# Two decode blocks on one core: eight units of K held over between the layers, and the weights in between streamed as one array

## The chip, the cores and the metric

The kernel runs on one core of a Trainium2 chip. The metric is the device time of one execution in microseconds (us); lower is better. The kernel before takes 2557.58 us, the median of three runs (2556.99 to 2559.53).

## The reference, cut to what matters

```python
def A(x, k_cache, v_cache, wq, wo):        # x (2, 1, 512); caches (2, 8, 32768, 128); all float32
    q = heads of x @ wq                    # 32 heads of 128; 4 heads share one K/V head
    p = softmax(q @ k_cache.T * 128 ** -0.5)
    return (p @ v_cache).reshape(2, 1, 4096) @ wo
def B(x, w_gate, w_up, w_down):            # 512 -> 1792 -> 512
    return (gelu(x @ w_gate) * (x @ w_up)) @ w_down
x = x + A(layernorm(x)); x = x + B(layernorm(x))
x = x + A(layernorm(x)); x = x + B(layernorm(x))     # the same caches and weights again
```

Both layers read the same K and V caches (268 MB each) and the same weights. One token per batch row is computed, so nearly all the work is reading.

## The kernel before

All data pass through one SBUF array, `mem`, of `UNITS` = 110 units. A **unit** is 512 float32 columns on 128 partitions: 262,144 bytes. Units 0 to 31 are region A, 32 to 63 region B, 64 to 95 region C, and 96 to 109 are the **room**. One (K/V head, batch row) pair has 64 units of K and 64 of V, and they are loaded as halves of 32 units. There are 16 pairs to a layer; the second layer visits them in reverse, so that the last pair of layer 0 is the first of layer 1.

All loads are issued on SP's queue from one list, `stream`, in the order in which it is filled. `plan` gives each load a fixed place in `mem`; `pump` (the DMA is line 487) issues the head of the list whenever its place is free; `done` and `give` free places as TensorE (PE) finishes with them. The wait of an SP instruction is thus a wait for the last reader of its place, and whatever is behind it in the list waits too. Line 716 is the score matmul, 782 the value matmul, 676 the query projection, 901 the gate/up matmul, 886 and 829 the down projection (829 also the last head of the output projection), and 641 (`warm`) a matmul on constants.

At the turn between the layers the last pair is not loaded again in full. Its V stays (64 units in B and C), its first 32 units of K stay in A, and `stash` (line 737) copies the last `WAIT` = 6 units of K out of region B into six PSUM banks, three copies on ScalarE (ACT) and three on VectorE (DVE), and `scores` copies them back to A (line 728) once part of A has been used. The other 26 units are loaded a second time:

```python
K_PARTS = [{}, {ORDER[-1]: [(32, 3), (35, 3), (38, 4), (42, 4), (46, 4), (50, 8)],   # (first unit, units)
```

Since A, B and C are full of kept data, everything between the layers goes through the room: the last 4 units of `wo`, gate and up (28 units in 8 pieces), `wd` (14 units in 4 pieces), `wq` of layer 1 (32 units in 10 pieces) and the first four K pieces. They rotate over four places of 3, 4, 3 and 4 units, so a piece can be issued when PE has used the piece four before it. Unit 96 is held for one half of the softmax result until `leave()`, after the values of the last pair. At the end of layer 1, regions A and C are free, and the 42 remaining units of weights are loaded ahead in larger pieces.

The last pair of a layer ends in `combine` (lines 793 and 794): ACT scales columns 0 to 255 of A's bank and DVE columns 256 to 511.

Of the kernel before, what the change touches and what calls it, by code (L numbers as in the profile page):

```python
# [12 lines left out]
OP = mybir.AluOpType  # L13
# [11 lines left out]
FH = 2 * KC * sum(FW)  # L25
FD = DF // P
HALF = 2048
# [21 lines left out]
BACK = A_AT + 13  # L49

K_PARTS = [{}, {ORDER[-1]: [(32, 3), (35, 3), (38, 4), (42, 4), (46, 4), (50, 8)],
# [7 lines left out]
WO_PARTS = [[(0, 28), (28, 4)], [(4, 28), (0, 4)]]  # L59
# [21 lines left out]

def plan():
# [12 lines left out]
    put("k", 1, last, [107, 96, 99, 103, A_AT, A_AT + 4])  # L95
# [3 lines left out]
    out["wq", 0, 0] = C_AT  # L99
    for i in range(10):  # L100
        out["wd", 0, i] = out["wq", 1, i] = [103, 106, 96, 99][i % 4]
    for i in range(8):
        out["gu", 0, i] = [103, 106.5, 96, 99][i % 4]
    out["wo", 0, 0] = out["wo", 1, 0] = C_AT
    out["wo", 0, 1] = 99
    out["wo", 1, 1] = 106
    for i, o in zip((0, 1, 4, 5, 6), (A_AT, A_AT + 7, A_AT + 14, A_AT + 21, A_AT + 24.5)):
        out["gu", 1, i] = o
    for i, o in enumerate((A_AT + 28, 97, 100, 104, C_AT)):
        out["wd", 1, i] = o  # L110
    return out
# [322 lines left out]
def block_kernel(nc, x, kt, vt, wq, wo, gu, wd, out):  # L434
# [76 lines left out]

    def meets(l, n):
        return (l == 0 and n == len(ORDER) - 1), (l == 1 and n == 0)
# [8 lines left out]
    for l in range(2):  # L522
        for i, (s, m) in enumerate(pieces(WQ_SPLIT[l])):
            add(("wq", l, i), wq[:, s * DM:(s + m) * DM], m * DM)
# [23 lines left out]
        if not l:  # L548
            add_wo(l, 1)
        for e in range(2):  # L550
            half_of = gu[e * P * FH:(e + 1) * P * FH].rearrange("(p c) -> p c", p=P)
            for j, (c, m) in enumerate(pieces(GU_SPLIT[l][e])):
                add(("gu", l, KC * e + j), half_of[:, c:c + m], m)
        for j, (o, m) in enumerate(pieces(WD_SPLIT[l])):
            add(("wd", l, j), wd[:, o * DM:(o + m) * DM], m * DM)
# [114 lines left out]
    def queries(l):  # L670
        qp = small(A)
        for j, (s, m) in enumerate(pieces(WQ_SPLIT[l])):
            w = get(("wq", l, j), m)
            for i in range(s, s + m):
                (k, v), t = divmod(i // 4, 2), i % 4
                pe.matmul(qp[32 * t:32 * t + 32, :], window(k, v), w[:, i - s, :],  # L676
                          start=(i < 4), stop=(i >= 8 * KC - 4))
                if i == 2:
                    spread(W if l else A)
            done(("wq", l, j))  # L680
            if l and j != len(WQ_SPLIT[l]) - 2:
                warm(256, W)
        for i in range(0, 512, 256):
# [14 lines left out]
    def scores(l, n, g, b):  # L698
# [3 lines left out]
        if second:  # L702
            todo = [(("k", 0, g, b, 0), s, s, m) for s, m in pieces(STEPS)] + [(None, BACK, 2 * CHUNK - WAIT, WAIT)]
        else:
            todo = []
        todo += [(("k", l, g, b, s), 0, s, m) for s, m in (parts if second else sorted_parts)("k", l, (g, b))]
        order = [j for key, o, s, m in todo for j in range(s, s + m)]
        for key, o, s, m in todo:
# [11 lines left out]
            if first:  # L720
                if s:
                    done(key, 0, m - WAIT)
# [108 lines left out]
    def last_head(l, g):  # L831
        s, m = WO_PARTS[l][1]
        w = get(("wo", l, 1), m)
# [21 lines left out]
    def feedforward(l):  # L855
# [22 lines left out]
        def down(j, n, m):  # L878
            w = get(("wd", l, j), m)
            for i in range(n, n + m):  # L880
                e, r = divmod(i, FD // 2)
                t, c = divmod(r, nj)
                h = hT[:, nj * e + c, t, :]
                if i < tops:
                    q = i % 4
                    pe.matmul(W[32 * q:32 * q + NB, :], h, w[:, i - n, :], start=(i < 4), stop=(i + 4 >= tops))
                    continue
                add_row(h, w[:, i - n, :], i == FD - 1)
            done(("wd", l, j))

        tops = sum(WD_SPLIT[l][:1 if l else 2])
        for e in range(2):
            for i, (s, m) in enumerate(pieces(GU_SPLIT[l][e])):
                key = "gu", l, KC * e + i
                w = flat_of(key)
                c = 0
                for k in range(KC):
                    for t, n in enumerate(FW):
                        if s <= c < s + m:
                            o = both[e][32 * t:32 * t + 32, :].rearrange("p (x c) -> p x c", x=2)[:, :, :n]  # L900
                            pe.matmul(o, window(k, 0), w[:, c - s:c - s + 2 * n].rearrange("p (x c) -> p x c", x=2),
                                      start=(k == 0), stop=(k == KC - 1))
                        c += 2 * n
                done(key)
                if e == i == 0:
                    spread(A)
                    rstd = state["rstd"]
                    hrr, cube, root = (tiny(n) for n in ("hrr", "cube", "root"))
                    dve.scalar_tensor_tensor(hrr, rstd, 0.5, rstd, op0=OP.mult, op1=OP.mult)
                    dve.tensor_scalar(cube, rstd, math.sqrt(0.044715), None, op0=OP.mult)  # L910
                    dve.tensor_scalar(root, rstd, math.sqrt(2.0 / math.pi), None, op0=OP.mult)
                if e and s + m == FH // 2:
                    hidden(0)
                if s + m == FH:
                    gelu(e)
                if e:
                    warm(256, W[:NB])
        n = 0
        for j, m in enumerate(WD_SPLIT[l]):
            if l and j == 1:  # L920
                hidden(1)
                turn(state["x"], side())
            elif not l and 1 <= j <= 2:
                if j == 1:
                    warm(256)
                    hidden(1)
                else:
                    warm(512)
                    turn(xin, side())
            down(j, n, m)  # L930
            n += m
# [51 lines left out]
_INS = ["x", "kt", "vt", "wq", "wo", "gu", "wd"]  # L983
# [6 lines left out]
def halves(gate, up):  # L990
    out = []
    for e in range(2):
        c, cols = e * DF // 2, []
        for n in FW:
            cols += [gate[:, c:c + n], up[:, c:c + n]]
            c += n
        w = np.concatenate(cols, axis=1).reshape(KC, P, -1).transpose(1, 0, 2)
        out.append(np.ascontiguousarray(w).reshape(-1))
    return np.concatenate(out)
# [27 lines left out]
```

## Time and profile before

| | |
|---|---|
| median of three runs | 2557.58 us |
| the profiled execution, whole | 2557.27 us |
| its span, first to last instruction | 2555.8 us |
| PE, DVE, ACT busy | 1228.2, 145.8, 81.4 us |
| read from HBM | 1102.58 MB, 431 GB/s over the span |
| DMA queue of SP | 99.9% of 16 engines' span |

The profile has one execution. Its span is 1.5 us shorter than that execution's time, and the execution is 0.3 us under the median. "DMA share" in the views below is the mean busy share of the core's 16 DMA engines; packets that overlap let it go a little above 1.

### The profile page before, as it was taken

To read this page: it belongs to the slowest core of one execution; us is meant where nothing else is said; L and a number is where in the kernel's file an instruction comes from. 1 tells how busy PE (TensorE), PEld (TensorE's weight loads), DVE (VectorE), ACT (ScalarE), POOL (GpSimd) and SP (SyncE) were. 2 spreads that over 40 slices of the span, in tenths; PEclk is the share of its full clock that TensorE was granted. 3 is DMA by queue.
4 is the path that set the end of the run, shared out by engine and by line. 5 is a ranking of instruction groups with operands and counts; after the bars stand their busy time and mean duration, and the time that the engine had idled before them with its cause. 6 is when DMAs were issued, how large, how long until landed. Compare 5 with 4: busy or idle time off the path is not lost.

```text
span 2555.8 us, 19801 instructions
## 1 busy us (share of the span) xinstructions
PE 1228.2 (48%) x9177; PEld 320.9 (13%) x9177; DVE 145.8 (6%) x495; ACT 81.4 (3%) x189; POOL 2.7 (0%) x9
## 2 busy tenths in 40 slices
PE   3444445354455354354684553544544544534456
PEld 1011111011011011111121110111111111101112
DVE  0000000000000000000010000000000000000001
ACT  0000000000000000000000000000000000000000
POOL 0000000000000000000000000000000000000000
PEclk8677777777777777776897767777777777767788
DMA  9999999999999999999999999999999999999999
GB/s 426 428 439 431 435 432 431 438 432 437 431 431 436 432 437 431 435 432 431 427 418 436 434 433 436 433 433 434 431 437 432 435 433 432 435 433 434 434 433 386
DMA packets 25091, 1102.91 MB, mean 432 GB/s; under 512 B 2792, under 2 KB 2928, under 8 KB 5616
## 3 DMA queue, kind: packets, MB, share of 16 engines
q1 hardware_dynamic: 25056, 1102.65, 99.9%
q8 instruction: 12, 0.20, 0.0%
q14 instruction: 7, 0.06, 0.0%
q10 hardware_dynamic: 16, 0.00, 0.0%
HBM read 1102.58 MB, written 0.07 MB: 431 GB/s over the span
## 4 chain that ended last, share of the span: by engine, by line
DMA 74%; PE 23%; SPq 1%; another core or an unknown queue 0%; DVE 0%; issue 0%; ACT 0%
DMA mem<-in_kt 37%; DMA mem<-in_vt 35%; PE S L716 12%; PE A L782 11%; DMA mem<-in_wd 1%; SPq L487 1%; DMA mem<-in_wq 1%; DMA mem<-in_gu 1%; PE A L676 0%; PE W L829 0%; PE A L716 0%; ACT T L753 0%; DVE desk L755 0%; DVE aux L719 0%
## 5 line engine op out<-in xcount | busy, mean ns | idle before, releaser
L716 PE MATMUL S<-mem,aux 128*32 128x512 f32 x4032 | 512.1, 666 | 617.3 <-DMA mem<-in_kt 617.3
L782 PE MATMUL A<-mem 128*16 128x512 f32 x2048 | 292.3, 732 | 477.6 <-DMA mem<-in_vt 477.6
L782 PE MATMUL A<-mem,desk 128*16 128x512 f32 x2048 | 286.2, 722 | 32.4 <-DMA mem<-in_vt 17.7
L716 PEld LDWEIGHTS S<-mem,aux 128*32 128x32 f32 x4032 | 133.7, 121 | 972.6 <-DMA mem<-in_kt 639.7
L782 PEld LDWEIGHTS A<-mem 128*16 128x16 f32 x2048 | 62.2, 113 | 705.5 <-DMA mem<-in_vt 507.6
L719 DVE TENSOR_REDUCE aux<-S 128x1 f32<-128x512 f32 x63 | 43.5, 691 | 1130.7 <-PE S L716 1130.7
L782 PEld LDWEIGHTS A<-mem,desk 128*16 128x16 f32 x2048 | 64.6, 111 | 227.4 <-issue 209.4
L753 ACT ACTIVATE T<-S,aux 128x512 f32<-128x512 f32 x63 | 41.4, 657 | 1196.7 <-DVE aux L749 1196.7
L759 PE MATMUL M<-aux 128*128 128x4 f32 x64 | 14.5, 298 | 85.2 <-DVE aux L757 85.2
L798 ACT ACTIVATE desk<-A,aux 128x512 f32<-128x512 f32 x30 | 20.6, 687 | 1072.2 <-PE A L782 1072.2
L803 DVE TENSOR_REDUCE aux<-A 128x4 f32<-128x64 f32 x16 | 3.6, 226 | 551.8 <-PE A L801 551.8
L803 DVE TENSOR_REDUCE aux<-M 128x4 f32<-128x64 f32 x16 | 3.6, 226 | 512.6 <-PE M L801 512.6
L746 PE MATMUL M<-aux 128*128 128x128 f32 x32 | 10.3, 323 | 34.5 <-DVE aux L744 34.5
L755 DVE STREAM_TRANSPOSE desk<-T 128x512 f32<-128x512 f32 x32 | 22.9, 716 | 27.0 <-ACT T L753 27.0
L759 PEld LDWEIGHTS M<-aux 128*128 128x128 f32 x64 | 11.7, 229 | 91.3 <-DVE aux L757 91.3
L755 DVE STREAM_TRANSPOSE mem<-T 128x512 f32<-128x512 f32 x32 | 22.9, 717 | 0.0
L811 PE MATMUL W<-mem,aux 128*2 128x512 f32 x112 | 16.8, 765 | 12.4 <-DMA mem<-in_wo 12.4
L641 PE MATMUL W<-aux 128*128 128x256 f32 (+3 forms) x58 | 18.0, 392 | 1.0 <-DVE W L876 0.7
L676 PE MATMUL M<-mem,aux 128*32 128x512 f32 x64 | 9.5, 669 | 18.0 <-DMA mem<-in_wq 18.0
L801 PE MATMUL A<-aux,desk 128*128 128x128 f32 x64 | 10.1, 280 | 14.6 <-ACT desk L798 13.7
L801 PE MATMUL M<-aux,desk 128*128 128x128 f32 x64 | 10.7, 287 | 12.8 <-ACT desk L798 12.3
L753 ACT ACTIVATION_READ_ACCUMULATOR T<-S,aux 128x1 f32 x63 | 12.4, 196 | 0.0
(136 smaller groups left out, 191.5 us busy)
## 6 DMA issues: line engine op xcount, KB each, us to landing
mem<-in_wo SPq DMA_DIRECT2D x2, 7168.0 KB
mem<-in_vt SPq DMA_DIRECT2D x3, 4096.0 KB, 20.0
mem<-in_vt SPq DMA_DIRECT2D x1, 6144.0 KB, 29.2
mem<-in_gu SPq DMA_DIRECT2D x6, 896.0 KB, 28.2
mem<-in_gu SPq DMA_DIRECT2D x3, 1792.0 KB, 40.2
mem<-in_kt SPq DMA_DIRECT2D x1, 4864.0 KB, 17.6
mem<-in_vt SPq DMA_DIRECT2D x2, 2048.0 KB, 32.4
mem<-in_wd SPq DMA_DIRECT2D x4, 1024.0 KB, 21.6
```

The source lines that it names most:

```text
L487: sp.dma_start(at[key][1], src, sem=(key[0], key[4]) if plain else "any")
L641: pe.matmul(bank, ident[:, :bank.shape[0]], part.to_broadcast([P, n]), start=alone, stop=alone)
L716: pe.matmul(banks[u][32 * t:32 * t + 32, :], pad[:, PAD_Q - 4 * c:PAD_Q + 32 - 4 * c], w[:, j - s, :], start=(j == tile_of[0]), stop=(j == ...
L719: dve.tensor_reduce(mx[:, u:u + 1], banks[u], axis=AX.X, op=OP.max)
L746: pe.transpose(m[:, :P], nm.to_broadcast([P, P]), ident)
L753: act.activation(T[u], banks[u], AF.Exp, bias=bias, scale=SCALE, accum_out=ls[:, u:u + 1])
L755: dve.transpose(p[u], T[u])
L759: pe.matmul(m[:, :REP], both.to_broadcast([P, P]), same, start=True, stop=True)
L782: pe.matmul(A[32 * t:32 * t + 16, :], p[u][:, at_p:at_p + 16], w[:, QUAD * i + t, :], start=(j == order[0]), stop=(j == order[-1]))
L798: act.activation(desk, A, AF.Copy, scale=linv)
L801: pe.transpose(m[:, c * P:(c + 1) * P], desk[:, c * P:(c + 1) * P], ident)
L811: pe.matmul(W[32 * t:32 * t + NB, :], heads(g)[:, t, :], w[:, REP * g + t - s, :], start=(g == turns[0]), stop=(g == turns[-1]))
```

## The change

- `stash` keeps eight units of K instead of six: the last `SPARES` = 2 units of `mem` (108 and 109) take two, copied from SBUF to SBUF, PSUM the other six. It makes eight copies, four on each engine, over two engines.
- The room that the pieces rotate in has `ROOM` = 12 units, in four places of 3. The second load of K is 24 units, as 3, 3, 3, 3, 4 and 8.
- The last four units of `wo`, gate/up, `wd` and `wq` become one array in HBM, `ws`, of 78 units a row. Between the layers it is read as 26 pieces of 3 units that pay no heed to where one matrix ends; the query weights at the very start come from it too. Gate and up are cut into units of 512 columns (`GU_UNITS`), in which the last, narrower block of two k-steps shares a unit.
- At the end of layer 1 the ten pieces are 7, 7, 7, 4, 3, 4, 3, 4, 2, 1 units (before 7, 7, 7, 3.5, 3.5, 4, 3, 4, 2, 1).
- `combine` for the last pair splits by partitions instead of columns: ACT takes 0 to 63, DVE 64 to 127, each with all 512 columns.

```diff
+ROOM = 12
+SPARE = ROOM_AT + ROOM
+SPARES = UNITS - SPARE
-K_PARTS = [{}, {ORDER[-1]: [(32, 3), (35, 3), (38, 4), (42, 4), (46, 4), (50, 8)],
+K_PARTS = [{}, {ORDER[-1]: [(32, 3), (35, 3), (38, 3), (41, 3), (44, 4), (48, 8)],
-WQ_SPLIT = [[32], [3, 4, 3, 4, 3, 4, 3, 4, 3, 1]]
-GU_SPLIT = [2 * [[1792, 1792, 1536, 2048]], [[FH // 2, FH // 2], [FH // 2, FH // 4, FH // 4]]]
-WD_SPLIT = [[3, 4, 3, 4], [4, 3, 4, 2, 1]]
+WO, GU, WD, WQ = 0, REP, REP + 2 * FD, REP + 3 * FD
+WEIGHTS = WQ + 2 * KC * REP
+SIZES = [3, 3, 3, 3]
+SPLIT = [(SIZES * 7)[:26], [7, 7, 7, 4, 3, 4, 3, 4, 2, 1]]
...
-        add_row(heads(g)[:, t, :], w[:, t, :], t == REP - 1)
-        done(("wo", l, 1))
+            w = get(("wo", l, 1), m)[:, t, :] if l else weight(l, WO + t)
+            add_row(heads(g)[:, t, :], w, t == REP - 1)
+            if not l:
+                spent(l, WO + t)
...
     def stash():
-        late = C_AT - WAIT
-        for bank, o, copy in zip(where, range(late, C_AT), 3 * [dve.tensor_copy, act.copy]):
-            copy(bank, mem[:, o * UNIT:(o + 1) * UNIT])
+        late = C_AT - WAIT - SPARES
+        key = "spare", 1
+        o = take(key, SPARES)
+        at[key] = (o, SPARES), mem[:, o * UNIT:(o + SPARES) * UNIT]
+        spots = [mem[:, (o + i) * UNIT:(o + i + 1) * UNIT] for i in range(SPARES)] + where
+        for spot, o, copy in zip(spots, range(late, C_AT), 4 * [dve.tensor_copy, act.copy]):
+            copy(spot, mem[:, o * UNIT:(o + 1) * UNIT])
         state["full"] = True
-        give(late, WAIT)
+        give(late, WAIT + SPARES)
...
-            act.activation(desk[:, :256], A[:, :256], AF.Copy, scale=linv)
-            dve.tensor_scalar(desk[:, 256:], A[:, 256:], linv, None, op0=OP.mult)
+            act.activation(desk[:P // 2], A[:P // 2], AF.Copy, scale=linv[:P // 2])
+            dve.tensor_scalar(desk[P // 2:], A[P // 2:], linv[P // 2:], None, op0=OP.mult)
```

On SP's queue, from the last pieces of V in layer 0 on, there stood before (elements per partition after the x; `s_6` is PE's semaphore, `s_4` and `s_8` those of DVE and ACT):

```order
L487 DMA mem<-in_vt 128x2048 [waits s_8,s_4] x2
L487 DMA mem<-in_wo 128x2048
L487 DMA mem<-in_gu 128x1792 x2
L487 DMA mem<-in_gu 128x1536 [waits s_6]
L487 DMA mem<-in_gu 128x2048 [waits s_6]
L487 DMA mem<-in_gu 128x1792 [waits s_6] x2
L487 DMA mem<-in_gu 128x1536 [waits s_6]
L487 DMA mem<-in_gu 128x2048 [waits s_6]
L487 DMA mem<-in_wd 128x1536 [waits s_6]
```

and now:

```order
L493 DMA mem<-in_vt 128x2048 [waits s_8,s_4] x2
L493 DMA mem<-in_ws 128x1536 x3
L493 DMA mem<-in_ws 128x1536 [waits s_6] x23
L493 DMA mem<-in_kt 128x1536 [waits s_6] x4
L493 DMA mem<-in_kt 128x2048 [waits s_6]
L493 DMA mem<-in_kt 128x4096 [waits s_6]
```

Behind the last V, 11 units (4 + 3.5 + 3.5) could be issued without waiting for PE; now it is 9 (three pieces of 3), and each later piece waits for PE as before.

On PE, from the end of layer 0 into the queries of layer 1 (829 and 845 are the down projection, 846/847 and 865/866 the residual, 653 and 666 the variance), there stood before:

```order
L829 MATMUL W<-mem,aux 2x128 x28
L641 MATMUL A<-aux 128x128
L846 MATMUL A<-aux,desk 128x16
L847 MATMUL A<-aux 128x8
L641 MATMUL W<-aux 2x128
L676 MATMUL A<-mem,aux 32x512 x3
L653 MATMUL W<-aux 128x8
L641 MATMUL W<-aux 128x256
L676 MATMUL A<-mem,aux 32x512 x4
```

and now:

```order
L845 MATMUL W<-mem,aux 2x128 x28
L654 MATMUL A<-aux 128x128
L865 MATMUL A<-aux,desk 128x16
L866 MATMUL A<-aux 128x8
L654 MATMUL W<-aux 2x128
L688 MATMUL A<-mem,aux 32x512 x2
L654 MATMUL W<-aux 128x256
L688 MATMUL A<-mem,aux 32x512
L666 MATMUL W<-aux 128x8
L688 MATMUL A<-mem,aux 32x512 x2
```

The piece that ends layer 0 now holds the last unit of `wd` and the first two of `wq`, so its place is freed two query units after the residual.

## Rows read from the trace of the kernel before

**Rows 1.** The page, part 4: the chain that ended last, by engine and line.
```profile
DMA 74%; PE 23%; SPq 1%; another core or an unknown queue 0%; DVE 0%; issue 0%; ACT 0%
```
**Rows 2.** Busy time by stretch, core 0: bulk, turn, its parts, bulk, end.
```profile
core 0: us, PE busy (x) PEld busy (x) DVE busy (x) ACT busy (x) POOL busy (x), PEclk, DMA share, GB/s
60.00:1255.00 1195.00, 555.10 (x4084) 141.01 (x4084) 62.56 (x206) 35.68 (x83) 0.00 (x0) 0.73 1.00 433
1280.00:1330.00 50.00, 38.89 (x316) 13.42 (x316) 5.98 (x28) 3.99 (x11) 1.10 (x2) 1.00 1.01 416
1288.00:1290.00 2.00, 1.06 (x6) 0.15 (x6) 0.14 (x3) 0.00 (x0) 0.00 (x0) 1.00 1.00 376
1330.00:1340.00 10.00, 9.28 (x82) 2.90 (x84) 3.71 (x8) 2.18 (x5) 0.00 (x0) 1.00 1.03 427
1380.00:2495.00 1115.00, 515.39 (x3818) 130.92 (x3818) 55.36 (x182) 30.47 (x71) 0.00 (x0) 0.73 1.00 434
```
**Rows 3.** The chain in order of time at the turn: start us, us, what.
```profile
1256.52 23.49 DMA mem<-in_vt
1280.05 1.10 PE A L782 x8
1281.17 0.48 ACT desk L793
1281.67 0.50 DVE desk L794
...
1283.19 1.10 PE W L829 x32
1284.29 0.02 issue
1284.31 6.99 DMA mem<-in_gu
1291.34 1.12 PE W L901 x7
1292.47 7.47 DMA mem<-in_gu
1299.99 1.12 PE A L901 x7
1301.12 7.54 DMA mem<-in_wd
1308.71 1.10 PE W L829 x32
1309.83 0.38 ACT desk L843 x2
...
1311.19 1.06 PE A L676 x6
```
**Rows 4.** DMA issues from 1258 to 1335 us: KB each, median us to landing.
```profile
mem<-in_wq SPq DMA_DIRECT2D x4, 1024.0 KB, 7.5
mem<-in_wq SPq DMA_DIRECT2D x5, 768.0 KB, 7.6
```
**Rows 5.** DMA issues from 2552 to 2556 us: the closing write.
```profile
out<-desk SPq DMA_DIRECT2D x1, 64.0 KB, 1.5
```
**Rows 6.** Timeline of ACT and DVE around the stash, and of PE afterwards.
```profile
1214.75 0.69 ACT L798 ACTIVATE desk<-A,aux 128x512 f32<-128x512 f32 x1 [36.67 <-PE A L782]
...
1253.11 0.72 DVE L755 STREAM_TRANSPOSE mem<-T 128x512 f32<-128x512 f32 x1
...
1254.55 0.59 ACT L737 COPY M<-mem 128x512 f32<-128x512 f32 x1
...
1255.80 0.68 DVE L737 COPY M<-mem 128x512 f32<-128x512 f32 x1
...
1285.60 1.06 PE L901 MATMUL W<-mem,aux 128*32 128x512 f32 x8
```

More of the change, by code (lines that the diff above doesn't have):

```diff
@@ L24 @@
 FW = (256, 256, 256, 128)
-FH = 2 * KC * sum(FW)
 FD = DF // P
+GU_UNITS = [[(k, t)] for k in (0, 1) for t in range(3)] + [[(0, 3), (1, 3)]]
+GU_UNITS += [[(k + 2, t) for k, t in unit] for unit in GU_UNITS]
 HALF = 2048
@@ L79, in sorted_parts, with weights @@
     return sorted(parts(*args))
+def weights(l):
+    return [(s + (GU if l else 0), n) for s, n in pieces(SPLIT[l])]
 def plan():
@@ L94, in plan @@
     put("v", 0, last, [C_AT, B_AT, B_AT + 16, B_AT + 24, B_AT + 28])
-    put("k", 1, last, [107, 96, 99, 103, A_AT, A_AT + 4])
+    room = [ROOM_AT + 3, ROOM_AT + 6, ROOM_AT + 9, ROOM_AT]
+    put("k", 1, last, [*room[2:], *room[:2], A_AT, A_AT + 4])
     put("k", 1, before, [A_AT + 19, A_AT, B_AT])
@@ L98, in plan @@
     put("v", 1, ORDER[0], [C_AT, B_AT, B_AT + 24])
[L99 to L105, printed above, removed]
-    out["wo", 1, 1] = 106
[L107 to L110, printed above, removed]
+    out["wq", 0, 0] = out["wo", 0, 0] = out["wo", 1, 0] = C_AT
+    out["wo", 1, 1] = 106
+    for i, (s, _) in enumerate(weights(0)):
+        out["w", 0, s] = room[i % 4]
+    for (s, _), o in zip(weights(1), (A_AT, A_AT + 7, A_AT + 14, A_AT + 21, A_AT + 25,
+                                      A_AT + 28, 97, 100, 104, C_AT)):
+        out["w", 1, s] = o
+    out["spare", 1] = SPARE
     return out
@@ L431, with block_kernel @@
 AUX = 440
-def block_kernel(nc, x, kt, vt, wq, wo, gu, wd, out):
+def block_kernel(nc, x, kt, vt, wo, ws, out):
     pr = Program(nc)
@@ L510, in add, with holder, weight, spent @@
         stream.append((key, src, cols))
+    def holder(l, u):
+        return next((s, m) for s, m in weights(l) if s <= u < s + m)
+    def weight(l, u):
+        s, m = holder(l, u)
+        return get(("w", l, s), m)[:, u - s, :]
+    def spent(l, u):
+        s, m = holder(l, u)
+        if u == s + m - 1:
+            done(("w", l, s))
+            return True
     def meets(l, n):
@@ L522, in block_kernel @@
     for l in range(2):
-        for i, (s, m) in enumerate(pieces(WQ_SPLIT[l])):
-            add(("wq", l, i), wq[:, s * DM:(s + m) * DM], m * DM)
+        if not l:
+            add(("wq", 0, 0), ws[:, WQ * UNIT:], (WEIGHTS - WQ) * UNIT)
         def halves_of(kind, n):
@@ L547, in block_kernel @@
                     add(*piece)
[L548 to L555, printed above, removed]
+        for s, m in weights(l):
+            add(("w", l, s), ws[:, s * UNIT:(s + m) * UNIT], m * UNIT)
     used = [0]
@@ L671, in queries @@
         qp = small(A)
[L672 to L681, printed above, removed]
+        for i in range(8 * KC):
+            w = weight(0, WQ + i) if l else get(("wq", 0, 0), 8 * KC)[:, i, :]
+            (k, v), t = divmod(i // 4, 2), i % 4
+            pe.matmul(qp[32 * t:32 * t + 32, :], window(k, v), w, start=(i < 4), stop=(i >= 8 * KC - 4))
+            if i == 2:
+                spread(W if l else A)
+            if l and spent(0, WQ + i):
                 warm(256, W)
+        if not l:
+            done(("wq", 0, 0))
         for i in range(0, 512, 256):
@@ L702, in scores @@
         if second:
-            todo = [(("k", 0, g, b, 0), s, s, m) for s, m in pieces(STEPS)] + [(None, BACK, 2 * CHUNK - WAIT, WAIT)]
+            todo = [(("k", 0, g, b, 0), s, s, m) for s, m in pieces(STEPS)] + [(None, BACK, 2 * CHUNK - WAIT, WAIT), (("spare", 1), 0, 2 * CHUNK - WAIT - SPARES, SPARES)]
         else:
@@ L721, in scores @@
                 if s:
-                    done(key, 0, m - WAIT)
+                    done(key, 0, m - WAIT - SPARES)
             elif key is None:
@@ L831, in last_head @@
     def last_head(l, g):
-        s, m = WO_PARTS[l][1]
-        w = get(("wo", l, 1), m)
+        s, m = WO_PARTS[1][1]
         for t in range(REP):
-            add_row(heads(g)[:, t, :], w[:, t, :], t == REP - 1)
-        done(("wo", l, 1))
+            w = get(("wo", l, 1), m)[:, t, :] if l else weight(l, WO + t)
+            add_row(heads(g)[:, t, :], w, t == REP - 1)
+            if not l:
+                spent(l, WO + t)
+        if l:
+            done(("wo", l, 1))
     def residual():
@@ L876, in hidden @@
                 dve.memset(m[:, :nj * P], 0.0)
[L878 to L917, printed above, removed]
@@ L918, in feedforward, with down @@
-        n = 0
-        for j, m in enumerate(WD_SPLIT[l]):
-            if l and j == 1:
-                hidden(1)
[L922 to L927, printed above, removed]
+        def down(i):
+            e, r = divmod(i, FD // 2)
+            t, c = divmod(r, nj)
+            h = hT[:, nj * e + c, t, :]
+            w = weight(l, WD + i)
+            if i < tops:
+                q = i % 4
+                pe.matmul(W[32 * q:32 * q + NB, :], h, w, start=(i < 4), stop=(i + 4 >= tops))
+            else:
+                add_row(h, w, i == FD - 1)
+            spent(l, WD + i)
@@ new lines, in feedforward @@
+        tops = 4 if l else 7
+        for u, blocks in enumerate(2 * GU_UNITS):
+            e, r = divmod(u, FD)
+            c = 0
+            for k, t in blocks:
+                n = FW[t]
+                o = both[e][32 * t:32 * t + 32, :].rearrange("p (x c) -> p x c", x=2)[:, :, :n]
+                pe.matmul(o, window(k, 0), weight(l, GU + u)[:, c:c + 2 * n].rearrange("p (x c) -> p x c", x=2),
+                          start=(k == 0), stop=(k == KC - 1))
+                c += 2 * n
+            ends = spent(l, GU + u)
+            if u == 2:
+                spread(A)
+                rstd = state["rstd"]
+                hrr, cube, root = (tiny(n) for n in ("hrr", "cube", "root"))
+                dve.scalar_tensor_tensor(hrr, rstd, 0.5, rstd, op0=OP.mult, op1=OP.mult)
+                dve.tensor_scalar(cube, rstd, math.sqrt(0.044715), None, op0=OP.mult)
+                dve.tensor_scalar(root, rstd, math.sqrt(2.0 / math.pi), None, op0=OP.mult)
+            if e and r == FD // 2 - 1:
+                hidden(0)
+            if r == FD - 1:
+                gelu(e)
+            if e and ends:
+                warm(256, W[:NB])
@@ L928, in feedforward @@
+        for i in range(FD):
+            if i == 4:
+                if not l:
+                    warm(256)
+                hidden(1)
+            if i == tops:
+                if not l:
                     warm(512)
-                    turn(xin, side())
-            down(j, n, m)
-            n += m
+                turn(state["x"] if l else xin, side())
+            down(i)
     def finish(l, n, p, linv):
@@ L980, in block_kernel, with blocks @@
     pr.emit()
-_INS = ["x", "kt", "vt", "wq", "wo", "gu", "wd"]
+_INS = ["x", "kt", "vt", "wo", "ws"]
 def groups(x):
     return np.ascontiguousarray(x.reshape(NB, HKV, P, NU // CHUNK, CHUNK * UNIT).transpose(0, 1, 3, 2, 4))
-def halves(gate, up):
+def blocks(gate, up):
     out = []
     for e in range(2):
[L993 to L999, printed above, removed]
+        for k, t in (x for unit in GU_UNITS for x in unit):
+            c = e * DF // 2 + sum(FW[:t])
+            out += [w[k * P:k * P + P, c:c + FW[t]] for w in (gate, up)]
+    return np.concatenate(out, axis=1)
 def kernel(A_x, A_k_cache, A_v_cache, A_wq, A_wo, B_x, B_w_gate, B_w_up, B_w_down):
@@ L1008 @@
     kc, vc = np.asarray(A_k_cache), np.asarray(A_v_cache)
+    wo = np.asarray(A_wo).reshape(HKV * REP, P, DM).transpose(1, 0, 2).reshape(P, HKV * HALF)
+    wq = np.asarray(A_wq).reshape(KC, P, 4, 2, DM).transpose(1, 0, 3, 2, 4).reshape(P, 2 * KC * HALF)
+    wd = np.asarray(B_w_down).reshape(FD, P, DM).transpose(1, 0, 2).reshape(P, FD * DM)
+    ws = [wo[:, -REP * DM:], blocks(np.asarray(B_w_gate), np.asarray(B_w_up)), wd, wq]
     arrays = {
@@ L1013 @@
                      .reshape(NB, HKV, P, NU, UNIT)),
-        "wq": f(np.asarray(A_wq).reshape(KC, P, 4, 2, DM).transpose(1, 0, 3, 2, 4)).reshape(P, 2 * KC * HALF),
-        "wo": f(np.asarray(A_wo).reshape(HKV * REP, P, DM).transpose(1, 0, 2)).reshape(P, HKV * HALF),
-        "gu": halves(np.asarray(B_w_gate), np.asarray(B_w_up)),
-        "wd": f(np.asarray(B_w_down).reshape(FD, P, DM).transpose(1, 0, 2)).reshape(P, FD * DM),
+        "wo": f(wo),
+        "ws": np.concatenate(ws, axis=1),
     }
```

2 lines of the change are left out of this document (1 added, 1 removed).

## The prediction

> **What bounds the kernel now.** I read the chain first: 74% of the span is DMA and 23% PE [rows 1]. Then the busy time by stretch: in both long bulk stretches the 16 DMA engines are busy all the time (share 1.00) and move 433 and 434 GB/s, while PE is busy for under half of it [rows 2]. So the bulk is bound by bytes: whatever engine work changes there costs nothing, and each byte not read is worth its time at 433 GB/s. The change acts at the turn between the layers, so I read that stretch by itself: from 1280 to 1330 us the engines are as busy (1.01) but move 416 GB/s [rows 2]. The reader should see two things there. The queue is not dry, so the turn too is bound by transfers, a little less efficiently. And there is one thin place, 376 GB/s from 1288 to 1290 us, so the cover is not unlimited. Last I read the chain in order of time through the turn [rows 3]. It alternates between a transfer of 7 to 7.5 us and 1.1 us of PE: a place of the room is freed, its next piece is issued, lands, is used, and the place is free again. That round is the thing which the change squeezes, from 14 units to 12.
>
> **The change, part by part.**
>
> *Bytes.* Six units of K were already kept in PSUM, so "eight" is two more than before. The second load of K goes from 3+3+4+4+4+8 = 26 units to 3+3+3+3+4+8 = 24. Two units are 524,288 bytes; at the 433 GB/s of the bulk [rows 2] that is **-1.21 us**. At the 416 GB/s of the turn it would be -1.26. The weights have the same 78 units at the turn and 42 at the end, so nothing else is saved. This is no more than 0.05% of the time, and I count only a difference of more than 0.2% (5.1 us) as one that a measurement of this kernel tells from no change.
>
> *Number of transfers.* The weights at the turn came in 1+8+4+10 = 23 pieces and now come in 26; the K pieces stay six, those at the end ten. A price for one more transfer comes from the turn: 50 us at 416 instead of 433 GB/s lose 50 x (1 - 416/433) = 1.96 us, over some 26 transfers that cross these 50 us (a piece of about 3.3 units lands every 2.1 us, with the dip counted in), so 0.08 us each. Three more: **+0.2 us**. From below the bound is 0; from above it is a transfer with nothing ahead of it and nothing beside it, the closing write, 1.5 us from issue to landing [rows 5], 4.5 us for three. I take the low value, because the transfers at the turn queue behind each other as these three will, and the closing write does not.
> The Trainium skill (DMA: Bandwidth & Descriptors, "Anatomy of one DMA — SWDGE (gpsimd) path") gives each DMA a fixed cost of about 2.0 us beside its bytes, measured on another issuing path, and its "Rules for kernel authors" ask for at least 1 MiB a transfer; both speak against 26 pieces of 768 KB. By that rule, with nothing overlapped, three more transfers would be +6.0 us and the sum 2562.4 us, an estimate from the page's figure. The rows do not bear that out for queued transfers: with 2.0 us each the turn could not reach 416 GB/s at a DMA share of 1.01.
>
> *The stash.* Eight copies instead of six: one more on ACT, 0.59 us by the copies there, and one more on DVE. That one goes from SBUF to SBUF, which no row shows; nearest are DVE's copy of the same shape out of `mem` (0.68) and its transpose into `mem` (0.72) [rows 6]; I take 0.7. The last pieces of V wait for it on SP, and all weights behind them: issued at about 1257.2 instead of 1256.5 us. The last V is the one issued at 1256.52, and it lands 23.5 us later [rows 3], because 28 units of V stand ahead of it in the queue, some 17 us at the bulk's rate. That covers it: **0**; +0.7 if the cover were gone.
>
> *The combine.* Now two halves of 256 columns in turn, from 1281.17 to 1282.17 us, DVE after ACT [rows 3]; then two halves of 64 partitions side by side. A scaling of 512 columns on ACT takes 0.69 [rows 6], so PE goes on about 0.3 us sooner. PE does not set the end of the turn, transfers do: **0**, at best -0.3.
>
> *The smaller room.* Here the change can lose. When the last V lands (1280.0 us), nine units of weights are behind it in the queue instead of eleven. The place of unit 96 is freed when the values end (1281.15), so there are 12 units, good for 7.56 us at 416 GB/s, to 1287.6. The next piece (the fifth) needs the place of the first, freed after three of four heads' rows: 1283.19, less 0.3, plus three quarters of 1.10 [rows 3], so 1283.7; with 1.5 us to start moving at the most [rows 5] it is there by 1285.2, 2.4 us ahead. The sixth piece needs the last unit of `wo` and the first two of gate/up. Gate/up starts at 1285.60 less 0.3 and takes 1.06 us for eight instructions [rows 6], two to a unit, so 1285.85; there by 1287.4, and the 15 units then queued last to 1289.5: 2.1 us ahead. In steady running a refill takes 1.5 us to start plus 768 KB at 416 GB/s (1.89 us) plus 1.1 us of PE, 4.5 us, against the 7.56 us that 12 units last: 3 us ahead. After the residual, the piece that holds the end of `wd` and the start of `wq` is held 1.4 us longer for it (1309.81 to 1311.19 [rows 3]): 1.6 us ahead. At the K pieces, 12 units instead of 14 stand in the room when the scores of layer 1 begin; that stretch now runs at 427 GB/s with share 1.03 [rows 2], so no gap is near. Everywhere the margin shrinks by 1.26 us and stays positive: **0**. From above: the dip at 1288 to 1290 us, which already loses 0.26 us (2 x (1 - 376/433)), says that these margins are not fully there; if it deepened by all of the 1.26 us, that would be +1.3.
>
> *The rest.* The first load of queries' weights has rows of the same 64 KB in a longer array; ten pieces at the end have the same sizes but for 4+3 instead of 3.5+3.5; the scores' 64 units are the same matmuls. 0.
>
> *Sum.* -1.21 + 0.2 = -1.0. The profiled execution took 2557.27 us, 0.3 under the median, so 2556.3 beside it, and beside the median of 2557.58: **2556.6 us**, no change that can be told.
>
> **The rivals.**
>
> *The ring is the limit (slower).* What if the round of the chain, 8.2 to 8.7 us from issue to issue (1284.31, 1292.47, 1301.12, 1309.83 [rows 3]), is not waiting in the queue but latency that stays? Then a round of 8.5 us brings 12 units instead of 14: 370 GB/s instead of 416. The turn's 78 + 12 units, 23.6 MB, would take 63.8 instead of 56.7 us: +7.1, and 2557.58 - 1.0 + 7.1 = 2563.7 us. For it: the chain is exactly this loop, and the dip exists. Against it: the share of 1.01, and that pieces of 1024 KB land in 7.5 us and pieces of 768 KB in 7.6 [rows 4], as things do that wait for the same queue and not for their own bytes. It decides once a refill with nothing ahead of it takes more than 7.56 us; I find 4.5.
>
> *Each transfer pays its own start (same).* Three times the 1.5 us of the closing write: 2557.58 - 1.21 + 4.5 = 2560.9 us. For it: only that the price is unknown. Against it: the dense queue above.
>
> *The title is meant in full (same, nearly faster).* If eight units were saved against the kernel before, 2.1 MB at 433 GB/s, -4.84: 2552.7 us. Against it: the sizes of the pieces in both tables.
>
> **How the numbers follow.** Forecast, with the dip's deepening in it: 0.82. Ring: 0.08. Own start: 0.05. Eight units: 0.01; a gain of over 0.2% that I have no mechanism for, such as a better order of reading in the one array: 0.04. The range takes the forecast's bounds, -1.26 - 0.3 and -1.21 + 0.2 + 1.3, and about what the runs of before lie apart around their median (-0.6 to +2.0): 2555.2 to 2559.9, widened a little to 2555.0 to 2560.0. Faster 0.04; slower 0.09, the ring and a margin that fails somewhere else; the same 0.87.
>
> **What would show it.** HBM read falls by 0.52 MB. At the turn the DMA share stays at 1.0 or more and the rate within a few GB/s of 416. Pieces of 768 KB land some 6.5 us after issue instead of 7.5, since less stands ahead of them. The stash shows four copies an engine, the combine two instructions side by side. The forecast is wrong if the share falls below 0.97 over the turn, or if the landings stay at 7.5 us, which would be the ring; or if the bulk's 433 GB/s moves.

## The result, and the profile after

The changed kernel takes **2562.91 us** (median of 17 runs, 2560.53 to 2565.64) against 2557.33 for the kernel before (17 runs beside them): 1.0022 times as long, 95% interval 1.0015 to 1.0029. It is slower by 5.6 us, just past the 0.2% that the prediction named, and 2.9 us above the range. The profiled execution took 2564.57 us, 7.3 more than that of before and 1.7 above its own kernel's median, so the rows below account for 7.3 us and not for 5.6.

The bytes came out as forecast, 0.52 MB fewer than the 1102.58 of before, and the bulk runs as in [rows 2]. By stretch, with the columns of [rows 2], the changed kernel:

```profile
60.00:1255.00 1195.00, 552.62 (x4084) 141.15 (x4084) 62.30 (x206) 35.65 (x84) 0.00 (x0) 0.73 1.00 433
...
1280.00:1330.00 50.00, 40.96 (x286) 13.94 (x286) 6.36 (x28) 3.98 (x10) 1.10 (x2) 0.93 0.92 345
...
1380.00:2500.00 1120.00, 521.07 (x3842) 132.80 (x3838) 56.11 (x183) 30.49 (x71) 0.00 (x0) 0.73 1.00 434
```

So it is the turn alone: 345 GB/s at a DMA share of 0.92, where before it was 416 at 1.01 [rows 2]. Pieces of 768 KB land 6.9 us after issue (the median from 1258 to 1335 us), between the 6.5 and the 7.5 that the prediction named. Cut finer, again the changed kernel and then, for the same stretches, the kernel before:

```profile
1280.00:1292.00 12.00, 9.57 (x86) 3.94 (x89) 1.98 (x11) 1.05 (x3) 0.56 (x1) 1.00 0.96 348
1292.00:1304.00 12.00, 8.63 (x54) 2.65 (x51) 2.33 (x7) 1.46 (x3) 0.00 (x0) 1.00 1.01 413
1304.00:1310.00 6.00, 5.44 (x58) 1.77 (x58) 1.50 (x6) 1.11 (x2) 0.00 (x0) 1.00 0.98 363
1310.00:1316.00 6.00, 4.33 (x44) 1.96 (x44) 0.37 (x3) 0.37 (x2) 0.00 (x0) 0.80 1.01 417
1316.00:1330.00 14.00, 12.99 (x52) 3.62 (x50) 0.17 (x2) 0.00 (x0) 0.55 (x1) 0.84 0.75 244
```

```profile
1280.00:1292.00 12.00, 8.65 (x89) 3.60 (x90) 1.60 (x11) 0.84 (x3) 0.55 (x1) 1.00 1.01 409
1304.00:1310.00 6.00, 4.61 (x85) 2.39 (x84) 0.25 (x2) 0.77 (x2) 0.00 (x0) 1.00 1.03 429
1316.00:1330.00 14.00, 11.21 (x61) 3.15 (x58) 0.00 (x0) 0.22 (x1) 0.00 (x0) 1.00 1.02 418
```

Twice the changed kernel runs at full rate with its 12 units (413 and 417 GB/s). In three places it does not: 12 x (1 - 348/409) = 1.8 us, 6 x (1 - 363/429) = 0.9 and 14 x (1 - 244/418) = 5.8 are lost, 8.5 together. Less the forecast's own 1.0 that is 7.5, and the two executions differ by 7.3. This is an estimate, since at one time the two kernels do not stand at the same piece, but it says where nearly all of the time went. What follows is why the queue thins there.

In each of the three places a piece holds a join in PE's work. The first has the end of `wo` and the start of gate/up, with the first residual between them; the last has the end of `wd` and the first queries, with the second residual. In the middle one PE transposes the first half of the hidden values (892) behind the seventh unit of the second half of gate/up, and that unit is the first of a piece of three:

```profile
1298.29 1.05 PE L916 MATMUL A<-mem,aux 128*32 128x256 f32 x4 [0.40 <-DMA mem<-in_ws]
1299.27 0.44 PE L892 MATMUL W<-aux,desk 128*128 128x128 f32 x2
1299.64 1.36 PE L916 MATMUL A<-mem,aux 128*32 128x512 f32 x5
```

This piece landed at 1298.25 us and the refill of its place was issued at 1300.73, 2.5 us later. In the kernel before a piece ends at each of these three joins.

The last place is the largest. PE's timeline of the changed kernel, from the last unit of the down projection (845) over the residual (865, 866) into the queries (688); start us, us, operation, and the idle time before it:

```profile
1312.43 0.40 PE L845 MATMUL W<-mem,aux 128*2 128x128 f32 x8 [1.03 <-DMA mem<-in_ws]
...
1313.59 0.58 PE L866 MATMUL A<-aux 128*128 128x8 f32 x2
1314.10 0.58 PE L654 MATMUL W<-aux 128*2 128x128 f32 x2
1314.50 1.92 PE L688 MATMUL A<-mem,aux 128*32 128x512 f32 x4
1316.35 1.22 PE L654 MATMUL W<-aux 128*128 128x256 f32 x2
1317.50 1.92 PE L688 MATMUL A<-mem,aux 128*32 128x512 f32 x2
1319.35 0.60 PE L666 MATMUL W<-aux 128*128 128x8 f32 x2
1319.88 1.27 PE L688 MATMUL A<-mem,aux 128*32 128x512 f32 x4
```

and by stretch:

```profile
1314.00:1316.00 2.00, 2.00 (x7) 0.35 (x7) 0.37 (x3) 0.00 (x0) 0.00 (x0) 0.50 1.01 421
1316.00:1318.00 2.00, 2.00 (x5) 0.69 (x4) 0.00 (x0) 0.00 (x0) 0.00 (x0) 0.50 0.75 209
1318.00:1320.00 2.00, 2.00 (x6) 0.63 (x6) 0.01 (x1) 0.00 (x0) 0.00 (x0) 0.50 0.82 326
1320.00:1322.00 2.00, 2.00 (x9) 0.51 (x12) 0.16 (x2) 0.00 (x0) 0.55 (x1) 0.91 0.04 15
```

The granted clock is 0.50 there: TensorE is at 1.2 GHz instead of 2.4. PE was busy all the time from 1314 to 1322 us and had waited twice for a transfer just before (1.03 us ahead of the last unit). Five units of queries take from 1314.50 to 1321.15. The pieces whose places they free are issued at 1316.46 and 1321.20, and from 1320 to 1322 the queue moves 15 GB/s.

### The profile page after: what moved, and what is told of

The parts are those of the page before. It is cut to its first block, busy times and chain, and to the rows that moved or that the text cites. A ratio compares the mean times of both kernels' runs of the same rounds, so it can differ in the third digit from the quotient of the medians.

```text
span 2563.1 us, 19829 instructions
## 1 busy us (share of the span) xinstructions
PE 1238.9 (48%) x9181; PEld 324.9 (13%) x9181; DVE 147.0 (6%) x496; ACT 82.2 (3%) x190; POOL 2.7 (0%) x9
## 4 chain that ended last, share of the span: by engine, by line
DMA 74%; PE 24%; SPq 1%; another core or an unknown queue 0%; DVE 0%; issue 0%; ACT 0%
DMA mem<-in_kt 36%; DMA mem<-in_vt 35%; PE S L728 12%; PE A L798 11%; DMA mem<-in_ws 3%; SPq L493 1%; PE A L688 0%; PE W L654 0%; PE W L916 0%; PE A L728 0%; PE W L845 0%; ACT T L769 0%; DVE desk L771 0%; DVE aux L731 0%
## 5 line engine op out<-in xcount | busy, mean ns | idle before, releaser
L688 PE MATMUL A<-mem,aux 128*32 128x512 f32 x64 | 14.6, 654 | 2.0 <-DMA mem<-in_ws 2.0
```

The costliest lines, as they stand in the source:

```text
L688: pe.matmul(qp[32 * t:32 * t + 32, :], window(k, v), w, start=(i < 4), stop=(i >= 8 * KC - 4))
```

## The experiments

Each is timed in 11 runs beside 33 of the kernel before (medians 2557.18 to 2557.32 in the four sets). They start from the changed kernel where nothing else is said.

**1. Hold the clock (e1_warm).**

```diff
-            spent(l, WD + i)
+            ends = spent(l, WD + i)
+            if ends and not l and i >= tops:
+                warm(256)
```

> Edit: the change, with one matmul on constants (256 columns, into bank A) behind each of the two pieces of the down projection of layer 0 that end after its seventh unit. In the changed kernel PE waits about 1.0 us for a transfer twice there, its granted clock falls from 1.0 to 0.5 at 1313.5 us for 6.8 us, the residual and the first five query units take 6.6 us instead of 2.9, two places of the room are freed 3 to 5 us late and the queue runs dry from 1317 to 1329 us. Theory A (the clock): with PE kept active the granted clock stays 1.0 through the turn, that gap goes, and some 4 to 5 us come back: 2558 to 2559 us against 2562.9. Theory B (12 units are too short by themselves): the time stays at 2562 to 2563 us, since no unit of room is added. Theory C (PE's order of gate and up is slower): also unchanged, its loss lies before 1292 us.

2561.88 us, ratio 1.0017 (1.0008 to 1.0026). PE's timeline at the same place:

```profile
1314.35 1.05 PE L688 MATMUL A<-mem,aux 128*32 128x512 f32 x4
1315.34 0.70 PE L654 MATMUL W<-aux 128*128 128x256 f32 x2
1315.97 1.05 PE L688 MATMUL A<-mem,aux 128*32 128x512 f32 x2
1316.94 0.39 PE L666 MATMUL W<-aux 128*128 128x8 f32 x2
1317.26 1.05 PE L688 MATMUL A<-mem,aux 128*32 128x512 f32 x4
1318.24 0.70 PE L654 MATMUL W<-aux 128*128 128x256 f32 x2
```

The clock held at this place and the five units end 2.8 us sooner, but the median fell by only 1.0 us, of 4 to 5 expected, with intervals that overlap. In this trace the clock fell at another place, to 0.79 on average from 1292 to 1300 us, so this run alone does not show what a full clock is worth. In the traces of `f1` and `h2` below it is 1.00 from 1280 to 1345 us, and those two executions, the quickest of their kernels, still take 2559.18 and 2559.96 us. Theory A is at most a part. The rows show another: at full clock a round of **two** instructions takes 1.05 us, as does one of four, and [rows 3] has one of six at 1.06. PE's time goes by rounds, not by units, and cutting five units into 2, 1 and 2, with side work between, costs three rounds.

**2. Give the room back (e2_room14).**

```diff
-ROOM = 12
+ROOM = 14
...
-SIZES = [3, 3, 3, 3]
+SIZES = [4, 3, 4, 3]
...
-        o = take(key, SPARES)
-        at[key] = (o, SPARES), mem[:, o * UNIT:(o + SPARES) * UNIT]
```

> Edit: the change without the two spare units: the room has 14 units again, in places of 4, 3, 4 and 3, K is loaded again from unit 32 in 26 units as before, and the one array still streams, now in 23 pieces. PE's order of work is that of the change but for where pieces end. Theory B (room): everything comes back, 2557.3 us or up to 0.3 more, and the DMA share stays at 1.0 through the turn. Theory A (clock): the time depends on whether the granted clock falls at the residual; if it still falls, PE takes the same 3 to 4 us more there, two more units (1.26 us) of cover catch a part, and the time is 2559 to 2562 us; if it stays at 1.0, 2557 to 2558. Theory C (order): the stretch up to 1292 us still shows a rate under 400 GB/s.

2557.88 us, 1.0004 (0.9995 to 1.0013): nearly everything is back, and the stream as one array costs nothing that can be told. In its trace the clock stays at 1.00 from 1280 to 1345 us and the rate is 412 GB/s. Its pieces of 4, 3, 4 and 3 units also end at all three joins again, so this run parts the room neither from the clock nor from the ends of the pieces.

**3. Gate and up in another order (e3_joint), and both (e4_warm_joint).**

```diff
-GU_UNITS = [[(k, t)] for k in (0, 1) for t in range(3)] + [[(0, 3), (1, 3)]]
+GU_UNITS = [[(k, t)] for k in (0, 1) for t in range(3)]
+GU_UNITS.insert(3, [(0, 3), (1, 3)])
```

> Edit: the change, with the unit that holds the last block of two k-steps moved from the seventh to the fourth place of its seven in gate and up. In the changed kernel twelve matmul instructions there take 1.90 us from 1287.40 to 1289.30, in the kernel before eight take 1.06. If four matmuls that write different groups of 32 PSUM rows run side by side and two that write the same group follow each other (theory C), the new place lets the narrow blocks run beside the others, gate and up of the first half take about 0.8 us less, the places are freed sooner and the rate up to 1292 us rises: 0.5 to 1.5 us less, about 2562 us. Theories A and B: no difference beyond what the clock does at the residual, 2561 to 2564 us.

> Edit: both of the last: the matmuls on constants behind the two pieces of the down projection, and the narrow unit in the fourth place. Theories A and C together: 4 to 5 us and 0.5 to 1.5 us come back, 2557 to 2558 us, and if nothing starves any more 2556.4. Theory B: 2561 us or more.

2562.67 us, 1.0022 (1.0013 to 1.0031), and 2561.42, 1.0017 (1.0008 to 1.0026). Theory C is a miss: the order inside gate and up is not what costs. In `e3`'s trace the clock stayed at 1.00 from 1310 to 1330 us without `e1`'s matmuls and fell to 0.79 on average from 1292 to 1300 us; its time is that of the changed kernel. So the fall is not tied to the second residual.

**4. Hold places for less time (f1_quick).**

```diff
-            if i == 2:
+            if i == (13 if l else 2):
                 spread(W if l else A)
-            if l and spent(0, WQ + i):
+            if l and spent(0, WQ + i) and i > 13:
                 warm(256, W)
...
-            if u == 2:
+            if u == (2 if l else 6):
                 spread(A)
```

> Edit: e1_warm, and PE's side work that sits inside the first pieces after a residual moved behind them: the variance matmul of gate/up from behind the third unit of layer 0 to behind the seventh, that of the queries of layer 1 from behind the third unit to behind the fourteenth, and no matmul on constants behind the first five query pieces. In e1_warm the query piece that starts at 1314.35 us and the next are done at 1318.3, because two units, a unit, two units and what lies between them each take a round of about 1.05 us; this edit makes it about 2.1 us sooner. Theory D (how long PE holds a place): a further 1 to 2 us come back, 2560 us. Theory B (units of room): 2561.5 to 2562 us, as e1_warm. If the granted clock falls in the queries, the gain is lost again.

2560.42 us, 1.0014 (1.0005 to 1.0023), with `e1_warm`'s matmuls in it. Five query units take 2.5 us (1313.37 to 1315.86) instead of 4.0 (1314.35 to 1318.31). The median falls by 1.5 us, the size that theory D gave, but not clear of the spread: the runs of the two kernels overlap (2559.18 to 2563.03, 2560.28 to 2563.40). The clock was 1.00 in its trace from 1280 to 1345, which it was not in `e1`'s, so the gain is not parted from the clock either. 3.2 us are still missing.

**5. Smaller places (f2_twos), and both (f4_twos_quick).**

```diff
-SIZES = [3, 3, 3, 3]
+SIZES = [2] * 6
-SPLIT = [(SIZES * 7)[:26], ...
+SPLIT = [(SIZES * 7)[:39], ...
...
```

> Edit: e1_warm with the same 12 units of room cut into six places of 2 units instead of four of 3: 39 pieces and six K pieces of 2; matmuls on constants behind every other piece. A place is freed after two units, so 10 units instead of 9 stand behind the one in use, as in the kernel before (10 to 11). Theory B in its form that counts the units in flight: about half of the loss comes back, 2559 to 2560 us, against 15 more transfers at 0.08 us, 1.2 us, so 2560 to 2561. Theory D: pieces of two units take a round of 1.05 us each as pieces of three or four do, so PE needs 1.05 us per 1.25 us of transfer, and it gets no better or worse: 2562 us or more.

> Edit: f2_twos and the moves of f1_quick together. If both the units in flight and the rounds on PE count, their gains add: 2558.5 to 2559.5 us; if only one does, as the better of the two. Best case, with nothing starving: 2556.1 plus 1.2 for 15 more transfers, 2557.3, no better than the kernel before.

2559.93 us, 1.0011 (1.0002 to 1.0020), and 2560.25, 1.0009 (1.0000 to 1.0018). Places of two bring back 2.0 us of `e1_warm`'s time although there are 15 more transfers. A place of two units is freed sooner, ten units stand behind the one in use, and no piece straddles a residual; this run does not part the three. The clock was 1.00 in its trace from 1280 to 1345 us. The two gains do not add.

**6. Thirteen units (f3_room13).**

```diff
-ROOM = 12
+ROOM = 13
...
-SIZES = [3, 3, 3, 3]
+SIZES = [4, 3, 3, 3]
...
```

> Edit: the change with one spare unit instead of two: a room of 13 in places of 4, 3, 3 and 3, seven units of K kept besides the 32, 24 pieces, K loaded again in 25 units. The first piece is now just the last head's four units, and ten units stand behind the last V. Theory B: a step between 12 (2562.9) and 14 (2557.9) units: 2559 to 2561 us. Theory D: the pieces that straddle a residual are others here (the first ends with the last head, so no place is held over the first residual), so nearly all comes back: 2557 to 2558 us. Theory A: by the granted clock at the second residual, 2557 if it stays and 2560 if it falls.

2557.41 us, 1.0002 (0.9993 to 1.0011): 5.5 us come back, as theory D said and more than theory B's 2 to 4. But two things changed. There is one unit more of room, and with places of 4, 3, 3 and 3 a piece now ends at each residual. The next experiment parts them.

**7. Room or ends of pieces (h1_align, h2_align_warm, h3_room13_across).**

```diff
 # h1, h2: 12 units, a piece ends with the down projection
-SPLIT = [(SIZES * 7)[:26], ...
+SPLIT = [[3] * 15 + [1] + [3] * 10 + [2], ...
...
 # h3: 13 units, pieces straddle both residuals
-SIZES = [4, 3, 3, 3]
+SIZES = [3, 3, 4, 3]
```

> Edit: the change (12 units, places of 3), but the sixteenth piece is cut to the one last unit of the down projection, so that no piece reaches across the second residual: 15 pieces of 3, one of 1, ten of 3, one of 2; one more transfer. The first residual is still straddled. Theory E (what the smaller room lost is mostly that a piece straddles the second residual, its place held for it and its two query units a round by themselves): 2559.5 to 2560.5 us, and the granted clock stays 1.0 there. Theory B (the units of room): 2562 to 2563 us, or more, since the piece of one unit leaves two units of its place empty just there.

> Edit: the last, with the matmuls on constants of e1_warm. Theory E: 2559 us, below e1_warm's 2561.9 by about 3. Theory B: as e1_warm, 2561.5 to 2562.5 us. If the granted clock was the whole difference between h1 and the change: equal to h1.

> Edit: f3_room13 with its places in the order 3, 3, 4, 3, so that pieces straddle both residuals again (the second piece has the last unit of the output projection and two of gate/up, a piece of 4 the last unit of the down projection and three of the queries); nine units or ten behind the last V, as 3, 3 and 4. Theory E: most of what f3 gained is lost, 2560 to 2561 us. Theory B: 2557.4 to 2558 us, as f3, since the room is the same.

`h3` takes 2561.25 us, 1.0019 (1.0010 to 1.0028). Its 11 runs (2560.08 to 2564.33) all lie above the 11 of `f3` (2556.80 to 2559.71): the same room and the same bytes, and 3.8 us more from where the pieces end, as theory E said; theory B is a miss here. Against the changed kernel, whose pieces straddle both residuals too, the one unit more of room is worth 1.7 us in the medians, and the runs of the two overlap. PE in `h3`, then the stretch 1312 to 1320 us in `h3` and in `f3`:

```profile
1311.21 0.40 PE L845 MATMUL W<-mem,aux 128*2 128x128 f32 x8 [1.64 <-DMA mem<-in_ws]
...
1313.05 1.93 PE L688 MATMUL A<-mem,aux 128*32 128x512 f32 x6
```

```profile
1312.00:1320.00 8.00, 7.67 (x28) 2.66 (x30) 0.54 (x5) 0.05 (x1) 0.55 (x1) 0.57 0.83 321
```

```profile
1312.00:1320.00 8.00, 6.64 (x37) 2.28 (x40) 0.54 (x5) 0.00 (x0) 0.55 (x1) 1.00 1.01 403
```

The last unit of the down projection now comes in a piece of four, so PE waits 1.64 us for it; then the granted clock falls, and the queue thins. In `f3` neither happens. Which of the two, the held place or the clock, carries the 3.8 us is not parted by this pair.

`h1` takes 2561.55 us, 1.0019 (1.0009 to 1.0028), and `h2` 2561.95, 1.0019 (1.0010 to 1.0028): with 12 units, a piece that ends at the second residual alone brings no difference that stands clear of the spread, so theory E does not hold there. In `h1`'s trace the clock fell all the same (0.83 on average from 1310 to 1330 us), in `h2`'s it did not, and both are slow from 1280 to 1292 us (355 and 360 GB/s), at the first residual, which they still straddle. The two traces are of executions 3.0 us above `h1`'s median and 2.0 below `h2`'s.

**8. How much lateness the kernel before stands (g1_late2, g2_late4).** From the kernel before, with n = 2 and 4:

```diff
         if l == 0:
             residual()
+            for _ in range(n):
+                warm(512, W)
```

> Edit: the kernel before (14 units of room), with two matmuls on constants of 512 columns between the residual of layer 0 and the queries of layer 1, so that PE frees the places there about 2 us later than it does. The prediction gave the smaller room 1.6 us of margin at this point and so the larger one 2.9: by that, no change, 2557.3 us. Theory B' (the margin is much smaller, since a transfer that is issued takes 1.0 to 1.8 us to its first packet even with an empty queue and lands some 2 us behind its first packets on the slowest of the 16 engines): 0.5 to 1.5 us more, about 2558.

> Edit: the same with four such matmuls, about 3.7 us. By the prediction's margin of 2.9 us: 0.8 us more, 2558. By theory B': as much as the first of the two and nearly all of the further 1.7 us, 2559.5 to 2560.5 us. The slope between this run and the last says what a microsecond of lateness of PE costs once the margin is gone.

2557.55 us, 1.0001 (0.9992 to 1.0010), and 2560.24, 1.0011 (1.0002 to 1.0020). The queries begin 1.8 us later than in the kernel before in `g1` (1312.94 us) and 3.5 us later in `g2` (1314.67 instead of 1311.19 [rows 3]). PE in `g2`, then the stretch 1310 to 1330 us in `g2` and in the kernel before:

```profile
1314.67 1.06 PE L676 MATMUL A<-mem,aux 128*32 128x512 f32 x6
```

```profile
1310.00:1330.00 20.00, 18.09 (x89) 5.96 (x88) 0.54 (x5) 0.12 (x2) 0.55 (x1) 1.00 0.96 363
```

```profile
1310.00:1330.00 20.00, 16.85 (x92) 5.11 (x90) 0.54 (x5) 0.42 (x3) 0.55 (x1) 1.00 1.02 416
```

So 14 units forgive 1.8 us of late freeing, and the next 1.7 us cost 2.7. Why they cost more than themselves stays open. The pieces end as before and the clock is 1.00 there: places that are freed late are enough to starve the queue, with no fall of the clock at this place.

**9. Towards a version that beats both (g3_room13_quick, g4_room13_warm, h4_room13_only_warm).** `f3` with `f1`'s moves, with `e1`'s matmuls too, and with `e1`'s alone.

> Edit: f3_room13 with the moves of f1_quick (variance matmuls behind the first pieces, no matmuls on constants behind the first query pieces). If the 13-unit room still loses about what PE's rounds cost, this is the version that beats both: 2557.25 less 0.6 us of bytes, 2556.7 to 2557.0. If the places are no longer what it waits for, no change from f3: 2557.4. If the granted clock falls in the queries for want of the matmuls on constants: 2558 to 2559.

> Edit: f3_room13 with the matmuls on constants of e1_warm and none of f1_quick's moves, which cost the granted clock in g3. If they hold the clock more surely and PE has time for them: 2557.0 to 2557.3 us, the best so far. If they only hold PE longer: 2557.5 to 2558 us.

2559.35 us, 1.0006 (0.9997 to 1.0015); 2558.88, 1.0006 (0.9997 to 1.0015); and 2557.59, 1.0001 (0.9992 to 1.0010). None beats the kernel before. For `g4` 2556.7 to 2557.0 was expected if the clock was what was left, else `g3`'s time or up to 0.3 us more; it came out like `g3`. `f1`'s moves cost 1.9 us with 13 units (`g3` beside `f3`), and 1.3 with `e1`'s matmuls (`g4` beside `h4`). In their traces the granted clock fell in the queries: on average it was 0.83 from 1310 to 1330 us in `g3` and 0.91 in `g4`, against 1.00 in `f3` and `h4`. That this fall is the whole cost is not shown. The whole turn, 1280 to 1345 us, in `f1`, `f3`, `g3` and `h4`, a fence each:

```profile
1280.00:1345.00 65.00, 54.52 (x411) 17.90 (x415) 10.07 (x36) 6.38 (x15) 1.10 (x2) 1.00 0.99 392
```

```profile
1280.00:1345.00 65.00, 53.66 (x422) 18.09 (x426) 10.06 (x36) 6.38 (x15) 1.10 (x2) 1.00 1.01 401
```

```profile
1280.00:1345.00 65.00, 54.11 (x406) 17.75 (x410) 10.07 (x36) 6.38 (x15) 1.10 (x2) 0.95 0.99 393
```

```profile
1280.00:1345.00 65.00, 55.52 (x438) 19.45 (x438) 10.06 (x36) 6.38 (x15) 1.10 (x2) 1.00 1.01 413
```

## Why the prediction was wrong

- *What bounds it*: right. Bulk and end did not move.
- *Bytes, -1.21*: the bytes are right, but no run sets them by themselves; 1 us does not show beside the rest.
- *Number of transfers, +0.2*: not set by itself, and nothing speaks against it. 26 pieces of 768 KB reach 413 and 417 GB/s where PE keeps up. The Trainium skill's fixed cost of about 2.0 us for each DMA (DMA: Bandwidth & Descriptors, "Anatomy of one DMA — SWDGE (gpsimd) path") does not add up between queued transfers here: `f2` has 15 transfers more than `e1` and takes 2.0 us less. That the prediction's estimate from it, 2562.4 us, comes near the result is luck.
- *The stash, 0*: right. The last V is issued 0.67 us later (0.7 forecast) and still lands after 23.2 us instead of 23.5. The new SBUF copy took 0.41 us, not 0.7:

```profile
1254.97 0.41 DVE L753 COPY mem<-mem 128x512 f32<-128x512 f32 x1
```

- *The combine*: side by side, as said; PE was 0.2 us sooner, of 0.3.
- *The smaller room, 0*: **this step failed**, in its margins.
  - "Gate/up starts at 1285.60 less 0.3 and takes 1.06 us for eight instructions [rows 6], two to a unit, so 1285.85". Gate/up started at 1285.94 and not at 1285.30, and I divided a round by its instructions. A unit or two takes the whole round of 1.05 us or more, so the place of the second piece, forecast free at 1285.85, was free and its refill issued at 1287.04, 1.2 us late and 2.9 us after the piece had landed (1284.14):

```profile
1287.04 0.33 SPq L493 DMA_DIRECT2D mem<-in_ws  x1
```

  - "A refill takes 1.5 us to start plus 768 KB at 416 GB/s (1.89 us)": 3.4 us. With the queue empty, from 1321 to 1322 us, the one issue of the changed kernel shows 4.2 from issue to landing:

```profile
mem<-in_ws SPq DMA_DIRECT2D x1, 768.0 KB, 4.2
```

  - "After the residual ... held 1.4 us longer ...: 1.6 us ahead." From the last unit of the down projection to the freed place took 4.0 us (1312.43 to 1316.46), and the next place was freed at 1321.2. I counted 1.1 us of PE and 1.4 for the residual, 2.5 in all, at the clock that the kernel before had. The straddling cut, the matmuls on constants and the variance that now sit between single query units, and the fall of the clock were not in it. The next place, and the one freed at 1300.73 us behind the transposition, I did not work out at all.
  - Together, as an estimate from these rows: 12 units last 7.56 us, and a refill of 4.2 us with the usual 1.1 of PE takes 5.3. With a place held for 4.0 us it takes 8.2, and the margin that I put at 1.6 us is gone.
  - `g1` and `g2` test the same margin in the kernel before, where the prediction's figures give 1.6 + 1.26 = 2.9. By that 3.5 us of lateness would lose 0.6; it lost 2.9.
- *The rivals*: the ring's time, 2563.7, was near the truth by luck; its mechanism was not right as it stood. It had every round slow, by a refill with nothing ahead of it that takes more than 7.56 us. In the trace 12 units suffice between the joins, where a round takes 5.3 by the estimate above, and fail at the three places where PE holds a piece too long. Own start, 1.5 us for each transfer, is refuted by `f2`: 15 more of them would have cost 22.5 us. Eight units is refuted by the bytes read.
- *The bounds*: +1.3 for a deeper dip was half of what the rows before 1310 us lost (2.7), and there was none for the rows behind (5.8). The lower end of the range adds up to 2555.4 and not 2555.2 (2557.58 - 1.56 - 0.6), which changes nothing. Of the signs of being wrong that it named, the first came true: the DMA share fell to 0.92 over the turn.

What stays open: how the 5.6 us divide among the units of room, the straddled joins and the clock. At 13 units the ends of the pieces were worth 3.8 us (`h3` against `f3`), with the held place and the fallen clock together in it. Lateness alone costs time even with 14 units (`g2`), and a full clock alone does not bring the time back (`f1`, `h2`). The three feed each other. No 12-unit kernel with three-unit pieces had a piece end at the first residual, and no 14-unit kernel had its pieces straddle. Each trace shows one execution, and the runs of one 12-unit kernel lie up to 5.3 us apart.

## What to carry to other kernels

A ring of buffers that runs at full rate is not yet a ring with margin: count for each slot how long its consumer holds it at the worst place, a reduction or a layer's end, in whole dependent rounds, add what a refill takes into an empty queue, and compare the sum with how long the rest of the ring lasts. When pieces of a stream are cut by size alone, look at which of them straddle such a place; here, with the same 13 units, that was worth 3.8 us, more than the bytes saved. A saving of 0.05% in bytes did not pay for a seventh of the room that covers PE's stalls.

## What the runs showed of the hardware

- Matmul instructions of this form (128x512 out of 32 columns) took 1.05 to 1.06 us at the full clock whether two, four or six stood together in a round (`e1`'s rows, [rows 3]), and 1.92 to 1.93 at 0.50 (the changed kernel and `h3`).
- The granted clock fell from 1.00 to 0.50 within the turn in some of the traces and not in others. Ahead of the fall PE had waited twice, 1.03 and 1.04 us, for pieces of the down projection in the changed kernel, and once 1.64 us in `h3`; in `g3` the matmuls on constants behind the first query pieces were missing. After it PE's rounds take 1.92 us, places are freed late, and the queue thins (15 GB/s from 1320 to 1322 us in the changed kernel).
- A transfer into an empty queue costs more than its bytes: 4.2 us for 768 KB (one case) that take 1.9 at the rate of the turn.
